# Chunk 1's decays read back from memory instead of built by TensorE, single loads per group, and a new instruction order

## The chip, the cores and the metric

One of the cores of a Trainium2 chip runs the kernel. The metric is the device time of one execution in microseconds (us). A core has five engines that run side by side, each through its own queue in order: TensorE (PE, matrix products), VectorE (DVE), ScalarE (ACT), GpSimd (POOL) and SyncE (SP), which here issues every DMA between memory and the on-chip buffers. Engines wait for each other on semaphores.

## The reference

Inputs are q, k, v and gates for 2 batches, 8 heads, 768 steps, head size 40. Three layers follow each other: a recurrent attention with a matrix state per head, and two small networks per token.

```python
for t in range(S):
    m_new = np.maximum(f_gate[:, :, t] + m, i_gate[:, :, t])
    f_stab = np.exp(f_gate[:, :, t] + m - m_new)
    i_stab = np.exp(i_gate[:, :, t] - m_new)
    C = f_stab * C + i_stab * outer(vt, kt)      # 40 x 40 state per head
    n = f_stab * n + i_stab * kt
    y[:, :, t] = sigmoid(o_gate[:, :, t]) * (C @ qt) / max(abs(n @ qt), 1)
# x: (2, 768, 320)
xn = (x - mean) / sqrt(var + 1e-06) * g_ln
x = x + relu(xn @ w_ch1) @ w_ch2                 # 320 -> 1280 -> 320
h = relu(x @ w_in)                               # 320 -> 1024
gate = sigmoid(conv3(h, conv_w))                 # along the sequence
out = (h * gate) @ w_out                         # 1024 -> 320
```

## The kernel before, in words

The 768 steps are cut into 6 chunks (c = 0 to 5) of 128. Within a chunk the recurrence is a masked attention: scores k·q (L488, two PSUM banks), multiplied by a decay matrix w (tile `wt`, 128 x 8 heads x 128) on DVE (L495), then the read-out (L504, L506), which adds the state `c` of the chunks before, applied to q times a decay `e` (tile `eg`). The state product of the next chunk (L541) uses k times `d`, the last column of w (POOL, L475). `attention(c, b)` records this for one chunk and batch b; "block" below is one such (c, b). Buffers rotate: 2 of `wt`, `eg` and `qt`, 3 of `vk` and `xy`.

The decays come from running sums of the gates. For chunk 0 they are made as the program starts. For chunks 1 to 5 `gates_rest` makes them in one go in tile `g80` (80 rows: 5 chunks x 16 heads and batches), and SP writes them to a scratch tensor `gd` in memory (L331, L332). How w and e are then made depends on the chunk:

- Chunks 0 and 1: PE builds log w in a PSUM bank by 6 matmuls per 4 heads, the "fill" (L434, L436, L438), and ACT takes exp of it in one instruction (L442).
- Chunk 1: PE spreads the rows of `g80` over 120 partitions by selector matrix `hsel` (L460), ACT takes exp (L464).
- Chunks 2 to 5: SP loads the rows of `gd` broadcast to 128 partitions, POOL masks them (L447), ACT takes exp head by head (8 x L451); e is loaded by three DMAs of 40 partitions and goes through one exp (L469). POOL multiplies q by e (L471).

After the read-out DVE normalizes (L516 to L533 give `xc`, ACT adds a small copy, L560), PE transposes (L567), ACT and DVE split the result into a high and a low part (`xth` L571, `xtl` L572). The first network is `f1_unit(c, u)`, u = 0 to 4: 16 matmuls L580 to L584, ACT's `uh` (L604), DVE's `ul` (L606), 12 matmuls L589 to L591. It needs both blocks of its chunk. The second network, `f2_unit`, does the same for chunk c - 3, with the convolution on ACT, DVE and POOL (L680 to L715). All weights come as 64-bit integers of doubles: SP loads 640 KB pieces into five staging buffers (`scr`, `stg`), ACT, DVE and POOL convert (L338 to L341) and split them into high and low parts (L364 to L386).

The order is written out by hand: `ORDER` lists the recorded operations by number, and each engine's queue is this list, cut to its own operations. A "-" is a dummy matmul on constants (L804, `warm`), which writes a PSUM bank that nothing reads. SP has 8 DMA slots in turn: a DMA is issued once the one issued 8 before it has landed, and once its buffer is free.

Of the kernel before, what the change touches and what calls it, by code (L numbers as in the profile page):

```python
# [8 lines left out]
F32 = mybir.dt.float32  # L9
# [21 lines left out]
10 8 41 9 5 11 6 30 - - 42 2 4 - 31 15 16 - 29 - 32 - 274 - 28 40 - 17 - 275 - - - - - 13 - - 3 86 39 7 - 18 - 14 20  # L31
273 53 157 93 107 - - 21 19 294 50 22 12 23 24 158 0 26 25 1 - 27 35 33 100 49 36 289 43 34 45 37 44 38 51 - 52 288 46
- - 87 56 47 88 89 48 54 280 286 55 - 90 67 58 59 57 60 68 91 114 61 62 94 63 - 159 69 64 70 95 92 380 108 287 71 65
109 121 72 66 96 73 97 - 160 173 101 74 - 162 - 75 381 102 163 - 237 - 98 76 172 - 238 165 171 161 80 77 166 239 78
164 81 240 99 167 83 241 - 84 - 379 - 82 116 - 242 168 128 169 79 276 115 179 85 170 281 103 277 117 104 300 110 278
282 295 283 105 243 123 106 111 296 244 122 135 301 279 124 245 297 284 400 246 290 402 112 302 403 247 175 285 291
113 129 118 292 130 131 142 248 293 137 249 125 303 298 119 250 132 126 304 120 251 127 133 - 508 - - - 509 143 252
255 149 305 144 253 306 174 299 136 180 134 254 308 176 145 187 177 138 178 146 150 307 404 321 139 322 147 323 414
152 151 148 182 153 256 382 140 324 392 261 181 309 310 325 257 141 262 154 311 258 188 330 326 312 263 259 507 155
327 313 189 194 260 383 318 264 267 401 314 319 405 386 268 315 389 320 391 156 409 265 269 316 394 528 343 266 412  # L40
393 270 317 344 384 395 345 333 328 407 346 271 334 331 347 329 390 335 348 336 410 332 272 337 388 338 417 422 341
408 415 423 387 339 416 342 190 340 396 183 191 349 413 530 406 531 385 350 411 397 398 420 192 425 355 424 418 399
351 356 419 195 352 426 196 193 197 357 353 716 421 208 428 354 717 427 198 361 358 429 184 199 185 200 367 209 510
431 186 520 210 362 215 211 201 432 368 212 433 363 434 364 430 369 435 213 370 511 436 437 214 373 513 532 512 542
517 440 515 438 229 518 374 443 439 529 444 441 519 516 445 442 514 455 375 359 446 523 456 376 526 452 522 202 527
447 521 360 203 533 453 217 365 715 448 216 457 366 449 204 541 471 538 450 371 536 472 534 218 451 473 372 539 454
537 219 540 461 535 458 544 462 377 459 545 463 550 543 474 378 460 548 475 220 476 549 464 524 467 477 465 469 525
468 230 466 478 221 736 232 470 551 231 546 205 479 483 739 553 738 552 484 547 206 480 554 207 485 486 481 902 555
233 903 556 495 222 234 557 235 558 728 559 560 561 718 562 563 224 564 223 565 568 740 571 566 489 750 572 569 567
737 573 570 583 490 584 574 731 719 225 729 580 491 730 496 722 575 721 226 727 585 901 482 726 581 497 576 725 589  # L50
741 498 723 487 590 577 492 724 599 488 746 600 578 601 742 745 582 493 602 749 744 743 591 494 751 603 747 604 752
758 499 748 753 579 756 720 757 586 732 500 587 733 734 920 588 501 227 735 502 754 228 592 755 503 605 593 504 606
594 236 759 607 608 505 923 760 922 761 621 506 622 623 637 595 624 596 611 597 638 625 598 626 762 612 627 628 631
613 629 614 639 632 763 640 765 615 633 641 616 764 642 617 643 618 827 634 766 914 767 619 768 904 769 770 771 772
647 924 779 773 780 774 934 781 776 775 782 648 620 921 777 649 783 905 663 778 788 664 630 912 925 784 911 916 910
789 679 915 913 785 790 909 917 813 930 791 680 786 657 936 814 933 937 650 787 815 792 699 935 927 651 816 929 793
794 652 817 658 918 818 653 795 846 654 919 797 796 940 700 655 659 926 801 660 665 609 932 666 938 673 667 906 939
907 668 674 908 669 928 931 610 635 644 645 636 646 670 671 656 681 675 672 682 676 661 683 701 684 702 689 685 662
686 865 690 687 677 691 692 688 693 678 694 695 705 696 697 703 802 706 803 704 798 804 707 799 698 807 800 708 808
825 805 709 806 941 710 711 712 884 826 943 713 819 942 828 829 714 944 830 809 811 810 831 812 844 945 832 845 946  # L60
833 947 847 1001 834 835 848 836 949 950 951 849 837 952 948 850 953 851 954 852 955 820 853 1020 958 956 854 957 863
821 959 960 822 967 855 961 968 969 856 962 963 973 838 964 965 987 966 839 988 989 990 970 991 840 992 864 971 841
823 972 866 867 882 883 868 869 976 885 824 977 870 842 978 974 871 857 975 872 1039 858 873 886 874 859 875 887 860
843 888 876 889 861 890 862 891 1058 892 877 893 878 879 894 880 983 985 984 895 986 896 993 897 898 994 999 995 996
1000 1012 1002 1003 1018 1004 1013 1005 1019 1014 1006 1015 881 1021 1007 1031 1008 1093 1032 1009 1022 1010 1011 1023
899 1024 900 1025 1026 1037 981 1027 1106 979 1038 982 1028 980 1075 1040 1079 1029 1041 1030 1042 997 1043 998 1044
1016 1045 1033 1046 1034 1017 1119 1047 1050 1051 1056 1052 1053 1057 1069 1076 1080 1077 1070 1059 1081 1078 1060
1082 1035 1061 1091 1062 1104 1063 1036 1064 1054 1065 1132 1071 1055 1066 1072 1092 1073 1094 1074 1105 1083 1095
1085 1117 1084 1107 1096 1086 1108 1118 1097 1146 1109 1120 1143 1130 1098 1110 1121 1131 1099 1111 1122 1155 1048
1100 1112 1144 1209 1049 1147 1145 1133 1168 1101 1148 1067 1134 1123 1166 1113 1135 1114 1124 1153 1136 1154 1192  # L70
1156 1125 1157 1210 1181 1137 1158 1068 1126 1138 1167 1127 1087 1159 1139 1088 1193 1169 1140 1089 1179 1170 1090
1160 1180 1171 1194 1223 1182 1161 1183 1236 1172 1212 1162 1237 1184 1173 1163 1195 1224 1174 1196 1249 1211 1197
1175 1225 1185 1176 1102 1226 1213 1198 1103 1186 1214 1115 1227 1116 1187 1215 1188 1238 1128 1199 1228 1189 1260
1239 1216 1164 1165 1240 1229 1217 1177 1200 1230 1178 1218 1201 1261 1190 1231 1250 1262 1219 1241 1191 1202 1232
1129 1242 1251 1141 1220 1252 1142 1253 1243 1203 1151 1233 1149 1152 1244 1204 1263 1150 1221 1222 1264 1245 1254
1246 1234 1207 1255 1265 1208 1205 1235 1256 1266 1206 1257 1267 1247 1258 1268 1248 1269 1259 1270 1271 1272 1274
1273 1275
"""


class Sched:

    LAT = {"A": dict(A=150, G=175, P=150, S=145, V=180), "V": dict(A=128, G=155, P=130, S=120, V=127),
# [786 lines left out]
```

## Time and profile before

| | us |
|---|---|
| median of 3 runs | 295.73 (293.85 to 297.31) |
| the profiled execution | 292.17 |
| its span, first to last instruction | 290.4 |
| PE busy in the span | 283.4 (98%) |
| DVE, ACT, POOL busy | 206.3, 179.0, 102.4 |

A page of the profile has the busy time of each engine, the chain of work that ended last, and groups of instructions by source line. PE's matmuls overlap each other, so that one shown with 0.28 us may follow its forerunner by 0.12; times between starts tell the rate. A view by windows gives busy times, TensorE's granted clock (1.00 is 2.4 GHz, 0.50 is 1.2 GHz) and DMA traffic in any stretch.

### The profile page before, as it was taken

Reading aid. Unit: us, or ns where it says so; the run is one execution under the profiler, and the core shown is the slowest. Engines: PE = TensorE matmul, PEld = TensorE weight load, DVE = VectorE, ACT = ScalarE, POOL = GpSimd, SP = SyncE. Lnnn points to the kernel's source line nnn. Section 1 sums busy time; section 2 is a strip of 40 time slices with the busy share of each in tenths; the row PEclk is TensorE's granted clock in tenths of the full one; section 3 lists DMA queues with packets and bytes.
Section 4 is the critical chain, followed back from the end, with each engine's and each line's share of the span. In section 5 each row is a group of like instructions: output and inputs, shape, how many; then the busy total and the mean of one; then the engine's idle time right before and its main releaser. Section 6 shows DMA issues by size and latency. Waiting matters only on the chain.

```text
span 290.4 us, 5879 instructions
## 1 busy us (share of the span) xinstructions
PE 283.4 (98%) x2206; PEld 269.0 (93%) x2209; DVE 206.3 (71%) x439; ACT 179.0 (62%) x409; POOL 102.4 (35%) x148
## 2 busy tenths in 40 slices
PE   8899999989999999999999999999999999999995
PEld 3685889979999999999999999999999999999995
DVE  4288987896798859469965678664165457899980
ACT  2376987878689638752685454463355447788861
POOL 6035767667537937500540000200000000444630
PEclk9997999999999999999999999999999999999999
DMA  7999888953698278022600010000100000010021
GB/s 180 279 380 271 279 234 290 292 208 83 208 313 292 59 240 273 27 56 96 212 14 1 2 47 1 0 2 0 47 0 2 0 0 3 1 47 1 2 90 45
DMA packets 13748, 33.27 MB, mean 115 GB/s; under 512 B 1783, under 2 KB 7688, under 8 KB 13720
## 3 DMA queue, kind: packets, MB, share of 16 engines
q1 hardware_dynamic: 13720, 32.90, 36.7%
q8 instruction: 17, 0.28, 0.4%
q14 instruction: 11, 0.09, 0.1%
HBM read 30.88 MB, written 2.01 MB: 113 GB/s over the span
## 4 chain that ended last, share of the span: by engine, by line
PE 85%; DMA 9%; ACT 1%; SPq 1%; issue 1%; DVE 1%; POOL 1%; POOLq 0%
PE bk L589 11%; PE bk L591 11%; PE bk L590 10%; PE bk L580 9%; PE bk L581 9%; PE bk L582 9%; PE bk L506 5%; PE bk L583 4%; PE bk L584 4%; DMA scr<-in_w_dram 4%; PE bk L488 4%; PE bk L504 3%; DMA vk<-in_vko_dram 3%; PE bk L567 3%; DMA wt<-gd 2%; PE bk L541 1%
## 5 line engine op out<-in xcount | busy, mean ns | idle before, releaser
L705 DVE SCALAR_TENSOR_TENSOR scr<-scr,cwr 128x256 f32<-128x256 f32 x70 | 35.8, 557 | 7.9 <-ACT scr L699 7.7
L680 POOL COPY scr<-scr 128x8 f32<-128x8 f32 (+1 forms) x21 | 6.0, 287 | 94.5 <-DVE scr L710 75.5
L589 PE MATMUL bk<-w2h,uh 128*128 128x320 f32 x120 | 38.3, 319 | 0.0
L591 PE MATMUL bk<-w2h,ul 128*128 128x320 f32 x120 | 37.2, 310 | 0.0
L590 PE MATMUL bk<-w2l,uh 128*128 128x320 f32 x120 | 37.1, 309 | 0.0
L580 PE MATMUL bk<-xth,w1h 128*128 128x256 f32 x120 | 35.7, 297 | 0.0
L581 PE MATMUL bk<-xth,w1l 128*128 128x256 f32 x120 | 33.8, 282 | 0.0
L582 PE MATMUL bk<-xtl,w1h 128*128 128x256 f32 x120 | 33.8, 282 | 0.0
L606 DVE SCALAR_TENSOR_TENSOR ul<-bk,uh 128x512 fp32r<-128x512 f32 x30 | 20.6, 687 | 17.5 <-ACT uh L604 17.3
L580 PE MATMUL bk<-rh,wih 128*128 128x256 f32 (+1 forms) x96 | 27.9, 291 | 0.0
L604 ACT ACTIVATE uh<-bk 128x512 fp32r<-128x512 f32 x30 | 17.9, 596 | 16.1 <-PE bk L584 13.9
L581 PE MATMUL bk<-rh,wil 128*128 128x256 f32 (+1 forms) x96 | 27.2, 284 | 0.0
L582 PE MATMUL bk<-rl,wih 128*128 128x256 f32 (+1 forms) x96 | 27.2, 283 | 0.0
L681 ACT ACTIVATE scr<-bk 128x512 f32<-128x512 f32 (+2 forms) x29 | 15.1, 522 | 17.5 <-PE bk L584 16.8
L506 PE MATMUL bk<-vk,wt 128*128 128x41 f32 x192 | 24.5, 270 | 0.0
L451 ACT ACTIVATE wt<-wt,bcol 128x128 f32<-128x128 f32 x64 | 21.4, 392 | 4.7 <-POOL wt L447 4.6
L506 PEld LDWEIGHTS bk<-vk,wt 128*128 128x128 f32 x192 | 24.1, 192 | 0.1
L341 POOL TENSOR_TENSOR scr<-scr 128x640 int32<-128x640 int32 x14 | 18.9, 1356 | 14.8 <-DVE scr L340 5.4
L589 PE MATMUL bk<-woh,uh 128*128 128x320 f32 x74 | 23.3, 315 | 0.0
L580 PEld LDWEIGHTS bk<-xth,w1h 128*128 128x128 f32 x120 | 22.6, 189 | 0.6
L589 PEld LDWEIGHTS bk<-w2h,uh 128*128 128x128 f32 x120 | 22.6, 189 | 0.4
L590 PE MATMUL bk<-wol,uh 128*128 128x320 f32 x74 | 22.9, 309 | 0.0
(192 smaller groups left out, 864.1 us busy)
## 6 DMA issues: line engine op xcount, KB each, us to landing
vk<-in_vko_dram SPq DMA_DIRECT2D x12, 528.0 KB
xy<-in_kq_dram SPq DMA_DIRECT2D x24, 192.0 KB
wt<-gd SPq DMA_DIRECT2D x8, 512.0 KB
scr<-in_w_dram SPq DMA_DIRECT2D x6, 640.0 KB
stg<-in_w_dram SPq DMA_DIRECT2D x4, 640.0 KB
scr<-in_win_dram SPq DMA_DIRECT2D x4, 640.0 KB
scr<-in_wout_dram SPq DMA_DIRECT2D x4, 640.0 KB
out_dram<-scr SPq DMA_DIRECT2D x12, 160.0 KB
```

The costliest lines, as they stand in the source:

```text
L341: op(G, 80 + 1.78 * n, [(rk, 0)], [(rk, 1)], lambda: gq.tensor_tensor(out=hi, in0=hi, in1=lo, op=ALU.add))
L451: lambda h=h: ac.activation(out=w[:, h, :], in_=w[:, h, :], func=AF.Exp, bias=bcol[:, c * 16 + r0 + h:c * 16 + r0 + h + 1]))
L506: pe.matmul(out=num[:, h * 41:(h + 1) * 41], lhsT=w[:, h, :], rhs=v1[:, h * 41:(h + 1) * 41], start=(c == 0), stop=(c == 0 or h == min(3 * ...
L580: pe.matmul(out=pv, lhsT=wh[:, k, fs], rhs=hi(k), start=(k == 0), stop=False)
L581: pe.matmul(out=pv, lhsT=wl[:, k, fs], rhs=hi(k), start=False, stop=False)
L582: pe.matmul(out=pv, lhsT=wh[:, k, fs], rhs=lo(k), start=False, stop=False)
L589: pe.matmul(out=a, lhsT=hi(b), rhs=wh[:, k, :], start=first, stop=False)
L590: pe.matmul(out=a, lhsT=hi(b), rhs=wl[:, k, :], start=False, stop=False)
L591: pe.matmul(out=a, lhsT=lo(b), rhs=wh[:, k, :], start=False, stop=last)
L604: op(A, da(512, True), [pk], [hk], lambda: ac.activation(out=uh[i], in_=pb, func=AF.Relu))
L606: lambda: ve.scalar_tensor_tensor(out=ul[i], in0=pb, scalar=0.0, in1=uh[i].bitcast(F32), op0=ALU.max, op1=ALU.subtract))
L705: ve.scalar_tensor_tensor(out=cvt()[:, j], in0=h[:, j, :, k:k + 128], scalar=cw_t[:, k, f0 + j:f0 + j + 1], in1=cvt()[:, j], op0=ALU.mult, ...
```

## The change

Chunk 1 now goes the way of chunks 2 to 5: w and e are loaded from `gd` (all conditions `c < 2` become `c == 0`). `hsel`, the second pair of `gp` and `bp` (inputs of the fill) and their making are dropped. For all chunks e is loaded by one DMA per group of three heads, to all 120 partitions; its source is three rows of `gd`, each repeated 40 times. The keys and queries of a block come by one load of 112 partitions instead of two of 48. Some durations that only served to find the order differ, and `ORDER` is a new list. Lines shift: L434 becomes L429, L447 L442, L451 L446, L469 L453, L488 L472, L567 L551, L580 L564, L804 L788.

```diff
--- before.py
+++ after.py
@@ -28,53 +28,53 @@
 ORDER = """
-10 8 41 9 5 11 6 30 - - 42 2 4 - 31 15 16 - 29 - 32 - 274 - 28 40 - 17 - 275 - - - - - 13 - - 3 86 39 7 - 18 - 14 20
...
+4 8 36 9 2 10 6 5 13 37 - - 28 - 26 25 3 - 27 - 153 - 81 - 11 0 - 7 12 1 - 265 - - - 95 14 - - - 15 44 16 - 152 - -
...
@@ -188,7 +188,6 @@
-    hsel = T([32, 17 * 40], "hsel")
...
@@ -270,20 +269,17 @@
...
-    op(G, 1500, ["ident"], ["hsel"],
-       lambda: gq.tensor_copy(out=hsel.rearrange("p (r d) -> p r d", d=40), in_=ident[0:32, 0:17].unsqueeze(2).to_broadcast([32, 17, 40])))
...
@@ -302,11 +298,11 @@
-        for t, src, sk, key in ((gp[k], g[0:16, :], gkey, ("gp", k)), (bp[k], i[0:16, :], ki, ("bp", k))):
-            op(A, da(L), [sk], [key], lambda t=t, src=src: ac.activation(out=t[0:16, :], in_=src, func=AF.Copy))
-            op(V, 200, [sk], [key],
-               lambda t=t, src=src: tv(out=t[32:48, :], in0=src, in1=t[0:16, :].bitcast(F32), op=ALU.subtract))
         if k == 0:
+            for t, src, sk, key in ((gp, g, gkey, "gp"), (bp, i, ki, "bp")):
+                op(A, da(L), [sk], [key], lambda t=t, src=src: ac.activation(out=t[0:16, :], in_=src, func=AF.Copy))
+                op(V, 200, [sk], [key],
+                   lambda t=t, src=src: tv(out=t[32:48, :], in0=src, in1=t[0:16, :].bitcast(F32), op=ALU.subtract))
@@ -412,7 +408,7 @@
-        load(v, vko[c, b], [("vk", vkey, x) for x in "vko"], 128 * VKO * 4.5)
+        load(v, vko[c, b], [("vk", vkey, x) for x in "vko"], 128 * VKO * 4)
         v1 = v[:, 0:VW]
         kk_ = v[:, VW:VW + KW]
         ot = v[:, VW + KW:VW + KW + DM]
...
@@ -421,11 +417,10 @@
         q, qk = qt[i % 2], ("qt", i % 2)
         e, ek = eg[i % 2], ("eg", i % 2)
         xt, xkk = xy[i % 3], ("xy", i % 3)
-        for h2 in range(2):
-            load(xt[64 * h2:64 * h2 + 48], kq0[c, b, h2], (xkk, h2), 48 * 4096)
-        if c < 2:
+        load(xt[0:112], kq0[c, b], [(xkk, h2) for h2 in range(2)], 112 * 4096)
+        if c == 0:
             for h2 in range(2):
-                wb = 6 if c else 4 + (2 * b + h2) % 3
+                wb = 4 + (2 * b + h2) % 3
                 bk = ("bank", wb)
                 wp = bank[wb].rearrange("p (h t) -> p h t", h=4)
 
@@ -433,15 +428,15 @@
                     r = r0 + h2 * 4
                     pe.matmul(out=wp, lhsT=identb, rhs=negm, start=True, stop=False)
                     for j in range(4):
-                        pe.matmul(out=wp[:, j, :], lhsT=sel[:, r + j:r + j + 1].to_broadcast([128, 128]), rhs=gp[c],
+                        pe.matmul(out=wp[:, j, :], lhsT=sel[:, r + j:r + j + 1].to_broadcast([128, 128]), rhs=gp,
                                   start=False, stop=False)
-                    pe.matmul(out=wp, lhsT=bp[c], rhs=sel[:, r:r + 4].unsqueeze(2).to_broadcast([128, 4, 128]),
+                    pe.matmul(out=wp, lhsT=bp, rhs=sel[:, r:r + 4].unsqueeze(2).to_broadcast([128, 4, 128]),
                               start=False, stop=True)
-                op(P, 216 * 2 + 4 * 97, [("gp", c), ("bp", c), "negm", "identb", "sel"], [bk], fw, act=0.8)
+                op(P, 216 * 2 + 4 * 97, ["gp", "bp", "negm", "identb", "sel"], [bk], fw, act=0.8)
                 op(A, da(512, True), [bk], [(wk, h2 * 4 + j) for j in range(4)],
                    lambda wp=wp, h2=h2: ac.activation(out=w[:, 4 * h2:4 * h2 + 4, :], in_=wp, func=AF.Exp))
         r1 = (c - 1) * 16 + r0
-        if c >= 2:
+        if c:
             load(w, gd[r1:r1 + 8, :].partition_broadcast(128), [(wk, h) for h in range(8)], 128 * 4096, reads=["gd"])
             op(G, 1060, [], [(wk, h) for h in range(8)],
                lambda: gq.affine_select(out=w, in_=w, pattern=[[0, NH], [1, L]], compare_op=ALU.is_ge, fill=NEG,
@@ -452,21 +447,10 @@
                                              bias=bcol[:, c * 16 + r0 + h:c * 16 + r0 + h + 1]))
         if c:
             load(q, q3t[c, b], qk, 120 * 3 * L * 4)
-            if c == 1:
-                gk, gb = pbank("sm")
-
-                def feg():
-                    for g in range(3):
-                        pe.matmul(out=gb[0:120, g * L:(g + 1) * L], rhs=g80[0:32], start=True, stop=True,
-                                  lhsT=hsel[:, 40 * (r1 + 3 * g):40 * (r1 + 3 * g + 3)])
-                op(P, 3 * 224 + 390, ["g80", "hsel"], [gk], feg, act=0.5)
-                op(A, da(384, True), [gk], [(ek, j) for j in range(3)],
-                   lambda: ac.activation(out=e, in_=gb[0:120, 0:384].rearrange("p (g t) -> p g t", g=3), func=AF.Exp))
-            else:
-                gsrc = gd[r1:r1 + 9, :].rearrange("(g j) t -> j g t", j=3)
-                for j in range(3):
-                    load(e[40 * j:40 * j + 40], gsrc[j].partition_broadcast(40), (ek, j), 2 * 40 * 3 * L * 4, reads=["gd", "gd8"])
-                op(A, da(384), [], [(ek, j) for j in range(3)], lambda: ac.activation(out=e, in_=e, func=AF.Exp))
+            for g in range(3):
+                gsrc = gd[r1 + 3 * g:r1 + 3 * g + 3, :].unsqueeze(1).to_broadcast([3, 40, L])
+                load(e[:, g, :], gsrc, (ek, g), 120 * L * 4, reads=["gd", "gd8"])
+            op(A, da(384), [], [(ek, j) for j in range(3)], lambda: ac.activation(out=e, in_=e, func=AF.Exp))
             op(G, dg(384), [(ek, j) for j in range(3)], [qk],
                lambda: gq.tensor_tensor(out=q, in0=q, in1=e, op=ALU.mult))
         if c < NC - 1:
```

The first place is PE from the transpositions of chunk 0 to the first matmul of the first network. Before (bk is a PSUM bank, `xc` a normalized block; further dummies are left out at "..."):

```order
L567 MATMUL bk_133<-ident,xc_104 128x128 x3
L541 MATMUL bk_132<-vk_85 120x123 x3
L567 MATMUL bk_134<-ident,xc_105 128x128 x3
L804 LDWEIGHTS const-bfloat16-1.0
L804 MATMUL bk_138<-const-bfloat16-1.0 128x512
...
L312 MATMUL bk_133<-ident,early_69 128x80
L434 LDWEIGHTS identb
L434 MATMUL bk_137<-ctmp,identb 128x512
L436 MATMUL bk_137<-xth_117 128x128 x4
L438 MATMUL bk_137<-xth_117 128x512
L460 MATMUL bk_134<-g_79,hsel 120x128 x3
...
L580 MATMUL bk_131<-xth_116,w1h 128x256
```

And with the change:

```order
L551 MATMUL bk_133<-ident,xc_104 128x128 x3
L788 LDWEIGHTS const-bfloat16-1.0
L788 MATMUL bk_137<-const-bfloat16-1.0 128x512
...
L551 MATMUL bk_132<-ident,xc_103 128x128 x3
...
L308 MATMUL bk_132<-ident,early_69 128x80
L564 MATMUL bk_130<-xth_115,w1h 128x256
L565 MATMUL bk_130<-xth_115,w1l 128x256
```

The fills and `hsel` products of chunk 1 are gone; 23 dummies now stand between the two transpositions (none before) and 7 behind the second (4 before). Up to the first matmul of the first network there are 71 dummies instead of 36.

The second place is SP from the write of `gd` to the end of chunk 1's reads, with the change (before, no read of `gd` was among them, and the first `wt` load stood nine rows behind the write):

```order
L327 DMA gd<-g_78 80x128
L328 DMA gd<-g_78 1x128
L251 DMA scr<-in_w_dram 128x1280 x2
L251 DMA vk_83<-in_vko_dram 128x1056
L251 DMA stg_119<-in_w_dram 128x1280
L251 DMA wt_90<-gd 128x1024
L251 DMA eg_88<-gd 120x1x128
L251 DMA wt_91<-gd 128x1024
L251 DMA eg_89<-gd 120x1x128
L251 DMA eg_88<-gd 120x1x128
L251 DMA eg_89<-gd 120x1x128 x2
L251 DMA eg_88<-gd 120x1x128
```

Eight loads of chunk 1's decays now stand between the weights of the first network and the first load of the second network's; the last of the six `eg` loads is the third one of `eg_88`.

The third place is ACT in the same stretch, with the change (`uh` is the first network's output, `stg` and `scr` are weights):

```order
L446 ACTIVATE wt_90<-wt_90,bcol 128x128 x6
L588 ACTIVATE uh_123<-bk_130 128x512
L446 ACTIVATE wt_91<-wt_91,bcol 128x128 x2
L457 ACTIVATE d_92<-wt_90 128x8
L453 ACTIVATE eg_88<-eg_88 120x384
L446 ACTIVATE wt_91<-wt_91,bcol 128x128 x6
L453 ACTIVATE eg_89<-eg_89 120x384
L457 ACTIVATE d_93<-wt_91 128x8
L360 ACTIVATE w1h<-stg_119 128x2x256
L588 ACTIVATE uh_124<-bk_131 128x512
L334 ACTIVATE stg_120<-stg_120 128x640
```

Where before two exps of 512 columns per block stood, there are now eight of one head each, and the exp of `eg_88` stands ahead of six of them, of weight conversions, and of what chunk 1's normalized blocks need from ACT.

## Rows read from the trace of the kernel before

**Rows 1.** Windows: us; busy PE, PEld, DVE, ACT, POOL; clock; DMA share; GB/s.

```profile
24.00:25.00 1.00, 1.00 (x3) 0.37 (x2) 1.00 (x5) 0.48 (x1) 1.00 (x1) 0.50 1.02 272
30.00:40.00 10.00, 9.88 (x75) 8.62 (x76) 9.50 (x13) 9.25 (x20) 8.73 (x7) 1.00 0.82 251
50.00:60.00 10.00, 10.00 (x84) 10.00 (x84) 9.14 (x21) 6.95 (x13) 6.45 (x6) 1.00 0.97 324
260.00:280.00 20.00, 20.00 (x147) 20.00 (x146) 18.96 (x31) 15.97 (x33) 10.80 (x11) 1.00 0.02 8
```

**Rows 2.** Chain of waits in order of time: start us, us, what.

```profile
34.93 1.09 PE bk L488 x16
51.65 6.95 DMA wt<-gd
66.70 0.31 PE bk L580
287.12 0.44 ACT scr L737
```

**Rows 3.** Timeline of PE: start us, us, line, operation, count, idle before.

```profile
0.84 6.63 PE L804 MATMUL bk<-const-bfloat16-1.0 128*128 128x512 bf16 x18 [0.84 <-PEq L860]
30.09 0.91 PE L460 MATMUL bk<-g,hsel 32*120 32x128 f32 x6 [0.18 <-DVE xtl L572]
30.94 0.39 PE L434 MATMUL bk<-ctmp,identb 128*128 128x512 bf16 x1
31.92 0.91 PE L460 MATMUL bk<-g,hsel 32*120 32x128 f32 x6
32.76 0.39 PE L580 MATMUL bk<-xth,w1h 128*128 128x256 f32 x1
43.25 0.82 PE L804 MATMUL bk<-const-bfloat16-1.0 128*128 128x512 bf16 x3 [0.16 <-issue]
44.86 0.31 PE L589 MATMUL bk<-w2h,uh 128*128 128x320 f32 x1
46.61 0.38 PE L504 MATMUL bk<-c,qt 120*128 120x123 f32 x2
61.65 0.44 PE L567 MATMUL bk<-ident,xc 128*128 128x128 f32 x2 [0.36 <-DVE xc L533]
62.76 0.33 PE L567 MATMUL bk<-ident,xc 128*128 128x128 f32 x1 [0.67 <-ACT xc L560]
```

**Rows 4.** Timeline of ACT, in the same columns.

```profile
18.80 0.69 ACT L364 ACTIVATE w1h<-scr 128x512 fp32r<-128x512 f32 x1 [1.18 <-POOL scr L341]
20.05 0.79 ACT L338 ACTIVATE scr<-scr 128x640 f32<-128x640 f32 x1
20.75 0.78 ACT L339 ACTIVATE scr<-scr 128x640 int32<-128x640 uint32 x1
28.87 0.80 ACT L339 ACTIVATE stg<-stg 128x640 int32<-128x640 uint32 x1 [0.66 <-DMA stg<-in_w_dram]
33.55 0.81 ACT L339 ACTIVATE scr<-scr 128x640 int32<-128x640 uint32 x1 [0.18 <-DMA scr<-in_w_dram]
67.02 1.26 ACT L451 ACTIVATE wt<-wt,bcol 128x128 f32<-128x128 f32 x4
```

**Rows 5.** DMA issues of the page: line, operation, count, KB each.

```profile
vk<-in_vko_dram SPq DMA_DIRECT2D x12, 528.0 KB
xy<-in_kq_dram SPq DMA_DIRECT2D x24, 192.0 KB
wt<-gd SPq DMA_DIRECT2D x8, 512.0 KB
scr<-in_w_dram SPq DMA_DIRECT2D x6, 640.0 KB
eg<-gd SPq DMA_DIRECT2D x24, 60.0 KB
```

**Rows 6.** Windows view, the columns of Rows 1, while six `eg` loads run alone.

```profile
62.00:63.00 1.00, 0.33 (x3) 0.24 (x3) 1.00 (x2) 1.00 (x5) 0.84 (x3) 1.00 0.42 130
```

## What the change does to the time: a prediction

> **What bounds the kernel now.** I read the windows first, then the chain of waits, then the timelines of PE, ACT and SP for the first 70 us. In the windows the reader is to see two stages. From 50 us on PE is busy but for one us near 62, 10.00 of 10 and 20.00 of 20 us in the windows shown, late on with DVE at 18.96 of 20 behind it and the granted clock at 1.00 (2.4 GHz) [rows 1]. Before that PE shares the bound with the loads: the DMA engines are 0.82 to 0.97 busy at 251 to 324 GB/s [rows 1], and PE fills gaps with dummies. The chain has its last links at 287.12, where PE hands over to the output copy [rows 2].
>
> The timeline of PE gives the marks that I use: first matmul of the first network at 32.76, read-out of chunk 1 from 46.61, transpositions of chunk 1 at 61.65 and 62.76 with 0.36 and 0.67 us of waiting [rows 3], and the first network's start on chunk 1 at 66.70 [rows 2]. From there to 287.12 are 220.4 us of PE work without a gap worth naming. The change leaves that work alone but for its order, so **the question is when chunk 1 reaches the first network**.
>
> **What goes.** PE loses four fills of 0.98 us (30.94 to 31.92) and two selector products of 0.85 (30.09 to 30.94) [rows 3], 5.6 us together. Two fills and both products stood ahead of 32.76, two fills behind it. ACT loses four exps of 512 columns, DVE and POOL some small preparations; they were beside PE's work and I give nothing for them.
>
> **What comes, ahead of the first network.** 35 more dummies at 0.215 us each (three in 0.82, the last of which shows 0.39 [rows 3]) make 7.5 us. Were all else as before, the first network would start at 32.76 - 3.7 + 7.5 = 36.6; dummies that only fill waits bring that down, by some 2 us at most, to 34.6. Now the chain: ACT reaches the small copy that the first transposition needs behind a conversion of `stg_120`. In the old queue 7,016 KB, summed along SP's rows, stand up to the load whose conversion starts at 28.87, freed by its landing [rows 4]; in the new one 7,092 KB stand up to `stg_120`. So: 29.1 landed, 0.8 conversion, 0.25 copy, transposition at 30.2, 0.3 for it, 23 dummies 4.9, second transposition 0.5, 7 dummies 1.5. **First network at 37.4**, 4.6 later. The far end: 18 dummies at the start took 6.63 us rather than 3.9 [rows 3], and in one stretch the clock stood at 0.50 (1.2 GHz) while dummies ran [rows 1]; if the 23 meet that, 2.8 more.
>
> PE then needs from 32.76 to 46.61, 13.85 us [rows 3], to chunk 1's read-out. The new queue holds there two fills less (2.0), 24 first-network matmuls (0.12 each) and 12 second-layer ones (0.146, from twelve in 44.86 to 46.61 [rows 3]) more, and one dummy more: 16.7. PE arrives at 54.1.
>
> **The read.** Up to `wt_90` SP's new queue holds 11,872 KB; 8,376 KB had landed at 33.5 before [rows 4, 5], and the 1,360 KB from 28.9 to 33.5 came at 303 GB/s. 3,496 KB more at that rate take 11.8 us: 45.3. At 251 and 324 GB/s [rows 1] it is 47.8 and 44.5. (The old first reads of `gd` took 6.95 us from issue [rows 2], with fewer loads ahead.) `wt_91` adds 512 KB, 1.75 us.
>
> The six `eg` loads in between are the unknown. While six old ones ran alone, the 16 engines were 0.42 busy at 130 GB/s [rows 6]: 6.7 engine-us for 254 rows of 512 bytes, 26 ns a row. A new load has 120 such rows. On all engines six cost 1.2 us; if each of the three source rows keeps to one engine, 40 rows take it 1.04 us, and six 6.2, during which every later load waits for these engines' share. The old source began with a dimension of 40 and kept less than half the engines busy; the new begins with 3. I take the upper end: **last `eg` at 45.3 + 1.75 + 6.2 = 53.3**; the lower is 48.3.
>
> The Trainium skill (page "DMA: Bandwidth & Descriptors", section "Why a DMA increments its semaphore by 16 and not by 1") says that a DMA is spread over the largest number of engines, up to 16, that divides the slowest dimension of both sides. By that rule the old loads had 10 engines and the new ones have 3, which would give the upper end; that less than half were busy agrees, and no run here shows the new form yet.
>
> **ACT behind it.** The exp of `eg_88` stands in ACT's queue ahead of everything that follows. Between it and the copy for chunk 1's normalized block come 8 exps at 0.29, 8 conversions at 0.70, two triple copies at 1.25 [rows 4], and five small ones, some 1.7 together: 12.1 us. 53.3 + 0.4 + 12.1 = 65.8; two copies, an exp and a first-layer output 1.1, two more exps and the two `xth` copies 1.4 with the transpositions between, DVE's last `xtl` 0.6: **first network on chunk 1 at 69.0**. PE would be there sooner: from 46.61 to 61.65 it took 15.0 with 40 and 36 matmuls of the two layers; with 16 and 12 it takes 8.7, so it arrives at 62.8 and waits some 4 us. That is the wait that takes the place of 1.03 us.
>
> One group of scores, 1.09 us [rows 2], stood ahead of 66.70 and now stands behind. **The sum**: 69.0 + 1.1 - 66.7 = +3.4 us on the profiled 292.17 (290.4 of span and 1.8 around it), 295.6. The median of the runs is 295.73, 3.6 above that execution, so I put the median at **299.1**.
>
> Costed at nothing: two more masks on POOL and 16 short exps less four long ones on ACT, counted where ACT binds; wider key loads, 12 of 448 KB for 24 of 192 KB [rows 5], whose 768 KB are in the byte sums early and lie under an idle DMA late (0.02 busy [rows 1]); without that cover they would cost 2.6 us in all. The `eg` loads of the later chunks meet idle engines too.
>
> **Rivals.** *The new `eg` loads are as wide as the old.* For it: same bytes, as many rows. Then `eg` is there at 48.3, ACT comes to it only after the first eight exps, near 51.5, and all behind moves up by 1.8: +1.6 us, 297.3, within 1%. Chance 0.30.
>
> *The removed PE work counts.* Against: the marks say that PE waits for loads and ACT. It decides if ACT has the copy of chunk 1's second block done by 60 rather than 66.9, which needs its conversions to run ahead in the waits I do not see. PE then goes 34.6 + 16.7 + 8.7 = 60.0, first network on chunk 1 at some 62: 62 + 1.1 - 66.7 = -3.6, 292.1, faster. Chance 0.10.
>
> *The tail turns into a wait.* The last convolution group's first matmul stands 72 closing matmuls from the end, 10.5 us at 0.146, where 114 or 16.6 us stood before, while DVE is 18.96 of 20 busy [rows 1]. A backlog of DVE as old would show as up to 4 us on top: 303. Chance 0.15, on the forecast's side. That the table is not used is excluded: the dummies stand where it has them.
>
> **How the numbers follow.** About 1%, 3 us, is what a measurement can tell from no change. Forecast 0.42 and tail 0.15 are slower by more: 0.57. The wide loads and a remainder of the forecast, within 1%: 0.33. Faster 0.10. The range leaves out the fast case below and the tail's end with a half-speed spell above: 294.2 to 303.2.
>
> **What would show it.** Right: first network at 36 to 39; the last `eg_88` near 53 with ACT waiting for it; PE waiting 2 to 5 us around 63 to 67; 220 us without a gap behind. Wrong: a landing of `eg` before 50, no PE wait ahead of the transpositions of chunk 1, or gaps in the last 20 us.

## The result: no difference that the runs can tell

The changed kernel takes 297.2 us (median of 20 runs, 293.92 to 303.38), the kernel before 296.15 (20 runs). The ratio, which leaves disturbed executions out and so is not the quotient of the medians, is 1.0062, 95% interval 1.0033 to 1.0091: 0.6% or 1.8 us, where 299.1 was forecast. Both kernels were run again, each time with a new comparison: the changed one gave 1.0021 [0.998, 1.0061] and 1.0080 [1.0034, 1.0127], the kernel before, against itself, 1.0055 [1.0005, 1.0105] and 1.0017 [0.9958, 1.0075]. So the unchanged kernel, too, shows half a per cent in one of two comparisons. The three ratios of the changed kernel have the mean 1.0054, the two of the unchanged one 1.0036. What is left is some 0.2%. All three ratios of the changed kernel lie within 1%, though the interval of the last one reaches 1.3%.

The profiled execution of the changed kernel took 296.33 us (span 294.5), 4.16 more than that of the kernel before, and this needs care (below). Its windows, in the columns of [rows 1]:

```profile
30.00:40.00 10.00, 9.76 (x43) 4.89 (x43) 6.17 (x15) 7.47 (x18) 5.35 (x10) 0.83 1.02 392
50.00:60.00 10.00, 10.00 (x91) 9.68 (x90) 7.53 (x15) 9.93 (x25) 7.05 (x8) 1.00 0.94 277
260.00:280.00 20.00, 20.00 (x157) 20.00 (x156) 15.99 (x29) 15.65 (x32) 10.71 (x13) 1.00 0.04 15
```

From 30 to 40 the DMA engines are full and move 392 GB/s where they moved 251 [rows 1], PE is at a mean clock of 0.83, and at the end PE is again without a gap.

The chain of waits from 14 to 38 us, in the columns of [rows 2]:

```profile
14.35 14.91 DMA stg<-in_w_dram
29.27 0.77 ACT stg L335
30.05 0.15 ACT xc L544
30.24 0.33 PE bk L551
30.57 6.69 PE bk L788 x23
37.26 0.34 PE bk L551 x3
```

The chain that the prediction drew is there: a weight load lands at 29.27, ACT converts it, then copies the small block, the transposition follows, and 23 dummies stand ahead of the second one. The timeline of PE, in the columns of [rows 3]:

```profile
30.24 0.33 PE L551 MATMUL bk<-ident,xc 128*128 128x128 f32 x1 [2.02 <-ACT xc L544]
30.41 6.85 PE L788 MATMUL bk<-const-bfloat16-1.0 128*128 128x512 bf16 x23
38.98 0.36 PE L564 MATMUL bk<-xth,w1h 128*128 128x256 f32 x1
55.13 0.45 PE L488 MATMUL bk<-c,qt 120*128 120x123 f32 x2
65.58 0.62 PE L551 MATMUL bk<-ident,xc 128*128 128x128 f32 x3 [0.43 <-DVE xc L517]
66.56 0.62 PE L551 MATMUL bk<-ident,xc 128*128 128x128 f32 x3 [0.36 <-DVE xc L517]
68.77 0.28 PE L564 MATMUL bk<-xth,w1h 128*128 128x256 f32 x1
69.69 0.39 PE L566 MATMUL bk<-xtl,w1h 128*128 128x256 f32 x1 [0.53 <-DVE xtl L556]
```

First network at 38.98, chunk 1's read-out at 55.13, first network on chunk 1 at 68.77. Ahead of the latter PE waits 0.43 and 0.36, just behind its start 0.53: 1.32 us, all for DVE. DVE itself works without a wait from 55 us on, so here its queue sets the pace. The timeline of ACT has no bracket, so no wait, at the exps of chunk 1's matrices (L446) and decays (L453), and POOL masks the first matrix at 44.98 without one:

```profile
29.27 0.77 ACT L335 ACTIVATE stg<-stg 128x640 int32<-128x640 uint32 x1 [2.97 <-DMA stg<-in_w_dram]
47.86 1.85 ACT L446 ACTIVATE wt<-wt,bcol 128x128 f32<-128x128 f32 x6
51.41 0.51 ACT L453 ACTIVATE eg<-eg 120x384 f32<-120x384 f32 x1
```

```profile
44.98 1.56 POOL L442 TENSOR_SCALAR_AFFINE_SELECT wt<-wt 128x1024 f32<-128x1024 f32 x1
```

**Three profiles of each kernel.** Two marks cut the span in three: the first matmul of the first network on chunk 0 and that on chunk 1 (66.63 in the first profile before, the piece at 66.70 in [rows 2]). Lengths in us, read from the timelines of PE:

```
                     start   to chunk 1   to PE's last matmul
before               32.76     33.87        220.46
  again              37.29     33.60        220.45
  third              35.56     33.55        221.75
  mean               35.20     33.67        220.89
changed              38.98     29.79        222.41
  again              40.01     29.79        221.76
  third              37.42     29.84        221.64
  mean               38.80     29.81        221.94
difference           +3.60     -3.86        +1.05    sum +0.79
```

The middle length hardly moves within a kernel, the start by 4.5 us. Three more profiles widen this. `eg_three` (below), which does the same as the changed kernel up to there, starts at 36.12. `xy_one` (below), which has the old order, has 34.19, 32.69 and 222.47. So the two kernels' starts overlap and the size of the +3.60 is uncertain by some us. The last length moves by 2 us within the old order (220.45 to 222.47), so the +1.05 is not told from scatter.

What makes the middle shorter can be counted. The groups of instructions between the marks (count, busy us, mean ns, idle before) have 48 score matmuls in the first profile before and 32 in the first one of the changed kernel:

```profile
L488 PE MATMUL bk<-xy 40*128 40x128 f32 x48 | 3.9, 287 | 0.0
L472 PE MATMUL bk<-xy 40*128 40x128 f32 x32 | 2.3, 285 | 0.0
```

One score group (1.1 us) has moved behind the second mark, and two fills (2.0 us) are gone. The rest of the 3.86, some 0.8 us, is not taken apart. (The 30.3 us of two expectations below are the same length, read to a matmul half a us later.) The profile from which the forecast was made had the earliest start of the three.

### The profile page after: what moved, and what is told of

The parts are those of the page before. It is cut to its first block, busy times and chain, and to the rows that moved or that the text cites. A ratio compares the mean times of both kernels' runs of the same rounds, so it can differ in the third digit from the quotient of the medians.

```text
span 294.5 us, 5891 instructions
## 1 busy us (share of the span) xinstructions
PE 285.0 (97%) x2208; PEld 265.1 (90%) x2208; DVE 204.5 (69%) x435; ACT 182.6 (62%) x419; POOL 102.3 (35%) x149
## 4 chain that ended last, share of the span: by engine, by line
PE 68%; DMA 13%; DVE 7%; ACT 6%; issue 2%; SPq 1%; POOL 1%; ACTq 0%; POOLq 0%
PE bk L573 9%; PE bk L575 9%; PE bk L574 9%; PE bk L564 7%; PE bk L565 7%; PE bk L566 7%; DMA stg<-in_w_dram 7%; PE bk L568 4%; PE bk L567 4%; DMA scr<-in_w_dram 3%; PE bk L490 3%; PE bk L551 2%; PE bk L788 2%; PE bk L472 2%; PE bk L488 2%
## 5 line engine op out<-in xcount | busy, mean ns | idle before, releaser
L689 DVE SCALAR_TENSOR_TENSOR scr<-scr,cwr 128x256 f32<-128x256 f32 x70 | 32.5, 509 | 14.0 <-ACT scr L683 12.4
L664 POOL COPY scr<-scr 128x8 f32<-128x8 f32 (+1 forms) x21 | 6.9, 330 | 86.2 <-DVE scr L694 82.7
L564 PE MATMUL bk<-xth,w1h 128*128 128x256 f32 x120 | 35.3, 294 | 0.0
L588 ACT ACTIVATE uh<-bk 128x512 fp32r<-128x512 f32 x30 | 17.7, 592 | 18.0 <-PE bk L568 14.6
L564 PE MATMUL bk<-rh,wih 128*128 128x256 f32 (+1 forms) x96 | 27.9, 291 | 0.0
L446 ACT ACTIVATE wt<-wt,bcol 128x128 f32<-128x128 f32 x80 | 26.4, 389 | 1.9 <-POOL wt L442 1.9
L337 POOL TENSOR_TENSOR scr<-scr 128x640 int32<-128x640 int32 x14 | 18.1, 1296 | 15.0 <-ACT scr L335 7.0
L575 PEld LDWEIGHTS bk<-w2h,ul 128*128 128x128 f32 x120 | 22.5, 188 | 0.9 <-DVE ul L590 0.9
L566 PEld LDWEIGHTS bk<-xtl,w1h 128*128 128x128 f32 x120 | 22.6, 188 | 0.7 <-DVE xtl L556 0.7
L564 PEld LDWEIGHTS bk<-xth,w1h 128*128 128x128 f32 x120 | 22.6, 188 | 0.6
```

The costliest lines, as they stand in the source:

```text
L337: op(G, 80 + 1.78 * n, [(rk, 0)], [(rk, 1)], lambda: gq.tensor_tensor(out=hi, in0=hi, in1=lo, op=ALU.add))
L446: lambda h=h: ac.activation(out=w[:, h, :], in_=w[:, h, :], func=AF.Exp, bias=bcol[:, c * 16 + r0 + h:c * 16 + r0 + h + 1]))
L564: pe.matmul(out=pv, lhsT=wh[:, k, fs], rhs=hi(k), start=(k == 0), stop=False)
L566: pe.matmul(out=pv, lhsT=wh[:, k, fs], rhs=lo(k), start=False, stop=False)
L575: pe.matmul(out=a, lhsT=lo(b), rhs=wh[:, k, :], start=False, stop=last)
L588: op(A, da(512, True), [pk], [hk], lambda: ac.activation(out=uh[i], in_=pb, func=AF.Relu))
```

## Experiments

Four repeats and eight variants were run; each ratio is to the kernel before, run at the same time.

**The kernels again.** No edit.

> The kernel before, unchanged, profiled a second time. Its first profiled execution took 292.17 us, less than the 20 timed ones (median 296.15). If the gap of 4.2 us between the two profiles is partly that execution's luck, this one comes out 1 to 3 us longer, with a difference to be seen ahead of 33 us (clock, first loads); if the gap is the change, span 290 to 291 again. Time ratio 1.00 within 0.5%.

> The kernel before a third time. Two profiles had the first network at 32.8 and 37.3 us and 254.3 and 254.1 us from there to TensorE's last matmul. Expected: the second figure 254 again, the first anywhere between 32 and 38; the ratio between 0.995 and 1.006.

> The changed kernel once more. If the change costs 0.6% and the comparison resolves that, the ratio is 1.003 to 1.009 again; if the comparison of two such kernels is itself uncertain by half a per cent (the unchanged kernel run under a new name came out at 1.0055), it can fall anywhere from 0.999 to 1.010. From the start of the first network to TensorE's last matmul this program should take 252 to 253 us as in its three other profiles, against 254.1 in both profiles of the kernel before; the start itself 36 to 39 us.

> The changed kernel a third time. Two profiles had the first network at 39.0 and 40.0 us and 252.2 and 251.6 us from there to the last matmul (30.3 us from network to network). Expected: these lengths again, the start between 36 and 40 us; the ratio between 1.000 and 1.009.

The ratios stand above, the spans were 294.7, 294.2, 294.9 and 292.2 us. So two executions of the same kernel differ by 4.3 us of span (290.4 and 294.7), as much as the two profiles that were to be compared, and all of it lies ahead of the first network. The traces show two causes.

In the second profile of the kernel before PE waits longer for the keys, and its granted clock then stands at 0.50 from 12 to 20 us (rows at the end):

```profile
10.67 1.80 PE L488 MATMUL bk<-xy 40*128 40x128 f32 x14 [1.13 <-DMA xy<-in_kq_dram]
37.29 0.39 PE L580 MATMUL bk<-xth,w1h 128*128 128x256 f32 x1
```

The fills of chunk 0 come slower, and ACT takes their last exp (L442) at 19.96, where it was 15.19 in the first profile. From there the lateness only travels on. The conversion that began at 28.87 in the first profile, freed by the landing of its load [rows 4], begins at 32.91 without a wait. ACT in the first profile (one row) and the second (two rows):

```profile
15.19 0.60 ACT L442 ACTIVATE wt<-bk 128x512 f32<-128x512 f32 x1 [0.29 <-PE bk L438]
19.96 0.60 ACT L442 ACTIVATE wt<-bk 128x512 f32<-128x512 f32 x1 [1.14 <-PE bk L438]
32.91 0.77 ACT L339 ACTIVATE stg<-stg 128x640 int32<-128x640 uint32 x1
```

In the third profile the last exp comes at 16.59, but the same conversion waits for its load until 31.46:

```profile
16.59 0.60 ACT L442 ACTIVATE wt<-bk 128x512 f32<-128x512 f32 x1 [0.39 <-PE bk L438]
31.46 0.79 ACT L339 ACTIVATE stg<-stg 128x640 int32<-128x640 uint32 x1 [1.17 <-DMA stg<-in_w_dram]
```

In the changed kernel, too, both play a part. In its third profile the 23 dummies (22 are recorded) take 5.19 us instead of 6.85, and the network starts 1.56 us sooner, though they begin at the same time:

```profile
30.51 5.19 PE L788 MATMUL bk<-const-bfloat16-1.0 128*128 128x512 bf16 x22
```

Some expectations were missed: the second profile before was 4.3 us longer, not 1 to 3, the second start of the changed kernel was 40.01, outside 36 to 39, with 251.6 us behind it instead of 252 to 253, and in the third profile before 255.3 us lie behind the start instead of 254.

**The removed TensorE work, in the new order** (`fills_kept`).

```diff
 program: that of the kernel before (fills, selector products, two key loads)
-ORDER of the kernel before
+ORDER of the changed kernel; fills and products of chunk 1 near its masks and exps
```

> The program of the kernel before (fills and decays of chunk 1 by TensorE, two loads per group) in the new order with its 75 dummies; the fills stand where the new order has the masks. Theory A (the removed TensorE work counts, the start is late for other reasons): the first network starts at 37 to 40 us or later by what is filled ahead of it, 254 us or more lie between it and the last matmul, and the time is 2 to 5 us over the changed kernel. Rival (the removed work lay beside waits of the same length): within 1 us of the changed kernel.

1.0165 [1.0092, 1.0238], median 300.2 us; the changed kernel had 1.0021 [0.998, 1.0061] against the same runs of the kernel before. The first network starts at 37.81, and 33.64 us lie between the marks. In the table it is 29.81 with the same order and the reads. So the new order alone does not shorten the middle; the removed work does, by 3.8 us, and that is what stands there. (It is not the make-up of the table's 3.86, since the old order has other work between the marks.) The view of instruction groups for PE in that stretch (count, busy us, mean ns, idle before) has three fills and one group of selector products; at 0.89 a fill and 0.91 they make 3.6:

```profile
L436 PE MATMUL bk<-xth 128*128 128x128 f32 x12 | 2.2, 308 | 0.0
L438 PE MATMUL bk<-xth 128*128 128x512 f32 x3 | 1.3, 432 | 0.0
L434 PE MATMUL bk<-ctmp,identb 128*128 128x512 bf16 x3 | 1.2, 390 | 0.0
L460 PE MATMUL bk<-g,hsel 32*120 32x128 f32 x6 | 0.9, 284 | 0.0
```

The rival (the removed work lay beside waits) falls. The key loads and the shape of the decay loads are old here as well; two runs below show no price of either.

**The reads, in the old order** (`order_old`).

```diff
 program: that of the changed kernel
-ORDER of the changed kernel
+ORDER of the kernel before; chunk 1's reads of gd behind its write, their masks and exps moved
```

> The changed program (chunk 1 read back, one load per group) in the order of the kernel before; only the reads of chunk 1 (right behind the write of the decays), their masks and exponentials and what hangs on them get new places. Theory A (the new order's lateness in front of the first network is what eats the saving): the first network starts near 30 to 33 us as in the kernel before less its two fills and two decay groups, and the time is 2 to 4 us under the kernel before. Theory B (the reads need the new order): ahead of the weights' loads they push the weights back, and their 16 exponentials (0.31 us apart on ScalarE) stand between the weights' conversions, so TensorE waits for chunk 1 or for weights by 50 us: time 1 to 5 us over the kernel before.

1.0278 [1.0182, 1.0374], median 306.95 us, more than theory B had it. Its profiled execution took 310.03 us, and much of its lateness lies ahead of the reads (its lines are one lower). SP issues no load between 14.47 and 31.79 us, the DMA engines stand at 0.01 from 24 to 32, PE's granted clock is 0.50 there, and the first read of `gd` is issued at 37.94:

```profile
24.00:32.00 8.00, 8.00 (x37) 7.41 (x37) 4.26 (x15) 3.97 (x7) 0.18 (x1) 0.50 0.01 3
```

Behind that comes the wait of theory B. ACT stands 4.95 us at an exp of `wt`, whose mask waits for the read; the first output of the network, `uh`, is behind it in the queue, and PE waits 6.73 us for that:

```profile
45.91 1.57 ACT L445 ACTIVATE wt<-wt,bcol 128x128 f32<-128x128 f32 x5 [4.95 <-POOL wt L441]
51.14 0.57 ACT L587 ACTIVATE uh<-bk 128x512 fp32r<-128x512 f32 x1
```

```profile
51.76 0.64 PE L572 MATMUL bk<-w2h,uh 128*128 128x320 f32 x1 [6.73 <-ACT uh L587]
```

With the runs above the four combinations are, as ratios to the kernel before (the diagonal as means of the repeats):

```
                     old order        new order
fills by TensorE      1.0036           1.0165
reads of gd           1.0278           1.0054
```

The new order costs some 1.3%, and the reads pay 1.1% back in it (the intervals reach 0.3% to 1% to either side). The reads in the old order cost 2.8%, but how much of that is theory B's wait and how much the stall ahead of it, is not shown: the old order with other places for the reads might do better.

**The shape of the decay loads** (`eg_three`).

```diff
-for g in range(3): load(e[:, g, :], gd[r1+3g:r1+3g+3, :].unsqueeze(1).to_broadcast([3, 40, L]), ...)
+gsrc = gd[r1:r1 + 9, :].rearrange("(g j) t -> j g t", j=3)
+for j in range(3): load(e[40*j:40*j + 40], gsrc[j].partition_broadcast(40), ...)
```

> The changed kernel with its decay loads in the shape of the kernel before (three loads of 40 partitions per group instead of three of 120 with a slow dimension of 3). Theory of the prediction (narrow loads hold the reads back): the last decays land 3 to 5 us earlier, ScalarE and TensorE wait less around 63 to 67, and the end comes 1 to 2 us earlier. Rival from the trace of the changed kernel (no exponential of chunk 1's decays waited for its load): end unchanged within 0.5 us, and the only wait on such a load (1.19 us at 74.6, chunk 2) goes or stays without moving TensorE.

1.0018 [0.9975, 1.0061]. Between the marks 29.81 us, as with the new loads: the rival that nobody waits for them. In the changed kernel (first row) the loads of the new shape run alone from 43 to 46. Loads of the old shape run all but alone in the kernel before (second row), in the busiest half us of the window of [rows 6], whose mean of 0.42 takes in time before they ran:

```profile
43.00:46.00 3.00, 3.00 (x23) 2.58 (x22) 2.09 (x4) 2.93 (x7) 2.23 (x2) 1.00 0.22 64
62.75:63.25 0.50, 0.49 (x4) 0.49 (x5) 0.50 (x2) 0.50 (x3) 0.34 (x2) 1.00 0.71 211
```

0.22 of 16 engines are 3.5 at 64 GB/s, 0.71 are 11.4 at 211 GB/s. The rule quoted from the Trainium skill (page "DMA: Bandwidth & Descriptors", section "Why a DMA increments its semaphore by 16 and not by 1") gives 3 and 10 engines; these traces agree in the ratio, and both shares come out some 15% high. At 64 GB/s the six loads, 368,640 bytes, take 5.8 us (6.2 forecast). So the loads are as narrow as forecast, and nobody waits for them: the last of their packets, by the trace's records the only ones of 512 bytes at that time, ends at 48.7, and ACT comes to them at 51.41. SyncE is longer at it, 8.05 us for five issues against 5.04 with the old shape (second row):

```profile
36.72 8.05 SPq L251 DMA_DIRECT2D eg<-gd  x5
34.56 5.04 SPq L251 DMA_DIRECT2D eg<-gd  x5
```

**The dummies** (`dummies_12`, `dummies_0`).

```diff
-transposition, 23 dummies, transposition, 7 dummies, first network
+transposition, 12 dummies, transposition, 7 dummies, first network     (dummies_12)
+transposition, transposition, first network                            (dummies_0)
```

> The changed kernel with 12 dummy matmuls instead of 23 between the two transpositions of chunk 0. In its trace xc of the first-in-queue batch is ready at 35.2 us, while the 23 dummies (6.85 us, from 30.4) hold TensorE until 37.1. Theory A (dummies in the way): the second transposition moves from 37.1 to about 35.3, the first network from 39.0 to about 37.2, and the end by 1 to 1.9 us: about 295.6 against 297.2. Theory B (they keep the clock): TensorE is at half clock longer and the first network runs in it: no gain, or up to 2 us lost. Theory C (chunk 1 sets the end anyway): the network starts 1.9 us earlier, but TensorE then waits as much longer at chunk 1's read-out or transpositions (54 to 67 us): end unchanged within 0.5 us.

> The changed kernel without any of the 23 dummies between and the 7 behind the transpositions of chunk 0. Theory A (in the way): nothing more than with 12 left, since the copy of xc at 35.2 us then sets the second transposition: first network at 36.5 to 37.2, end 1 to 2 us earlier. Theory B (they keep the clock): TensorE stands idle from 30.4 to 35.2, the granted clock is at half when the first network starts, and its first 3 to 4 us of matmuls take twice as long: first network past its first unit no earlier than in the changed kernel, end 0 to 3 us later than it. Theory C: end unchanged within 0.5 us, the gain lost at 54 to 67 us.

With 12: 1.0029 [0.9978, 1.0080], start 37.37, 29.75 us between the marks. With all 23 it was 37.42 to 40.01, and 36.12 in `eg_three`; the second transposition now waits 1.04 and 0.47 us for `xc`. Whether 11 dummies cost anything is not shown. With none: 1.0130 [1.0065, 1.0196], 298.04 us: theory B, clear of `eg_three` in the same comparison. PE idles 3.67 us; then the network's matmuls take 0.41 us instead of 0.28 and stand at a granted clock of 0.50 (1.2 GHz) for 8 us, and 33.22 us lie between the marks, 3.4 more (its lines are one lower):

```profile
34.41 0.69 PE L550 MATMUL bk<-ident,xc 128*128 128x128 f32 x2 [3.67 <-DVE xc L516]
37.12 0.56 PE L563 MATMUL bk<-xth,w1h 128*128 128x256 f32 x1
43.84 0.41 PE L564 MATMUL bk<-xth,w1l 128*128 128x256 f32 x1
44.86 0.28 PE L564 MATMUL bk<-xth,w1l 128*128 128x256 f32 x1
```

```profile
36.00:44.00 8.00, 7.00 (x38) 6.56 (x39) 2.34 (x6) 4.23 (x8) 4.85 (x5) 0.50 0.72 274
```

**An earlier start** (`chain_first`, `chain_gap`), the attempt to keep the saving and get the start back.

```diff
 VectorE, ScalarE, chunk 0's second block:
-readout, conversions, gate, statistics, conversions, xc, conversions; copy of xc behind a weight's conversion
+readout, gate, statistics, xc, conversions; copy of xc ahead of it                       (chain_first)
+readout, conversion, gate, statistics, xc, conversions; copy of xc behind two of them    (chain_gap)
 TensorE: 8 and 4 dummies (chain_first), 2 and 3 (chain_gap) in place of 23 and 7
```

> The changed kernel with chunk 0's second output chain (readout, gate, statistics, xc, its copy) put ahead of the weights' conversions on VectorE and ScalarE, and 8 and 4 dummies in place of 23 and 7. In the changed kernel ScalarE stood 2.97 us for a weight load ahead of a copy of xc, and VectorE 1.84 us behind it. Theory A (the chain waits behind conversions that wait for loads): both transpositions by 32 us, first network at 32 to 34 us, the end 2 to 4 us earlier than the changed kernel. Theory B (the weights themselves arrive no earlier): TensorE waits 2 to 6 us for w2 at the network's first second-layer matmuls (38 to 45 us), end within 1 us of the changed kernel.

> The changed kernel with four instructions of chunk 0's second output chain (gate, two of statistics, xc) moved on VectorE into the 1.84 us in which it waited for a conversion of ScalarE, its copy and transposition behind them, and 2 and 3 dummies in place of 23 and 7; no conversion is moved behind a wait (that is the difference to the run in which the chain went ahead of all of them). Theory A (every us by which the first network starts earlier is kept, since 30.3 us lie between the two networks in all profiles of the changed program): first network at 33 to 34 us instead of 39 to 40, no new wait behind it, the end 3 to 5 us earlier: 292 to 294 us. Theory B (ScalarE's conversions set the pace): TensorE waits 2 to 5 us between 37 and 46 us at the first second-layer matmuls, and the end stays within 1 us of the changed kernel. Half clock at the start of the network may take 1 us of A.

1.0224 [1.0160, 1.0288] and 1.0119 [1.0037, 1.0200]. In the same comparisons the changed kernel had 1.0021 [0.998, 1.0061] and 1.0080 [1.0034, 1.0127]: the first is slower than it, the second not faster, though the network starts at 34.58 and 36.02. The middle grows to 42.0 and 35.2 us. In the first, ACT waits 3.54 us for the moved `xc` and converts the weights behind it later, and PE waits 4.44 us at the second layer:

```profile
32.64 0.26 ACT L544 ACTIVATE xc<-xc 128x64 f32<-128x64 f32 x1 [3.54 <-DVE xc L517]
33.70 0.77 ACT L335 ACTIVATE stg<-stg 128x640 int32<-128x640 uint32 x1
45.60 0.57 ACT L588 ACTIVATE uh<-bk 128x512 fp32r<-128x512 f32 x1
```

```profile
46.22 0.41 PE L573 MATMUL bk<-w2h,uh 128*128 128x320 f32 x1 [4.44 <-ACT uh L588]
```

In the second, ACT reaches the first `uh` (L588, first row) at 42.02 without a wait, its queue being full up to there. In the changed kernel (second row) it is there at 42.40 after waiting 1.19 us for PE, which began 3 us later:

```profile
42.02 0.58 ACT L588 ACTIVATE uh<-bk 128x512 fp32r<-128x512 f32 x1
42.40 0.60 ACT L588 ACTIVATE uh<-bk 128x512 fp32r<-128x512 f32 x1 [1.19 <-PE bk L568]
```

PE then waits 0.89, 0.91 and 2.14 us:

```profile
48.18 0.41 PE L575 MATMUL bk<-w2h,ul 128*128 128x320 f32 x1 [0.89 <-DVE ul L590]
55.96 0.46 PE L488 MATMUL bk<-c,qt 120*128 120x123 f32 x2 [0.91 <-DVE wt L479]
68.36 0.55 PE L551 MATMUL bk<-ident,xc 128*128 128x128 f32 x3 [2.14 <-ACT xc L544]
```

These are the waits of theory B: a start that PE alone gets is taken back by queues behind it, ACT's above all. But theory B had the end within 1 us of the changed kernel, and the first attempt is some 6 us over it: moving the chain also made the conversions later. Fewer dummies may have a part in both (the clock is 0.68 and 0.50 from 32 to 36), which was not tested apart. Theory A, and my expectation of 292 to 294 us, fall.

**The key loads alone** (`xy_one`).

```diff
 kernel before, its order
-for h2 in range(2): load(xt[64*h2:64*h2 + 48], kq0[c, b, h2], (xkk, h2), 48 * 4096)
+load(xt[0:112], kq0[c, b], [(xkk, h2) for h2 in range(2)], 112 * 4096)
```

> The kernel before, in its own order, with one part of the change alone: the keys and queries of a group in one load of 112 partitions (448 KB) instead of two of 48 (384 KB together). Theory of the prediction (no term: hidden): within 0.3% of the kernel before. Rival 1 (a load on more partitions comes in sooner): the second scores start 0.5 to 1.5 us earlier than 9.0 to 10.7 us and so does the first network. Rival 2 (17% more bytes in a stretch in which the transfers are never idle): the weights' loads come 0.2 us later per group, the first network 0.5 to 1 us later.

1.0040 [1.0001, 1.0080], hardly more than the unchanged kernel's 1.0036. The second scores wait 2.25 us and start at 10.65, so they are not sooner:

```profile
10.65 1.38 PE L486 MATMUL bk<-xy 40*128 40x128 f32 x16 [2.25 <-DMA xy<-in_kq_dram]
```

That the part is hidden is borne out as far as half a per cent can tell.

## Why the prediction was right, and where not

- **Range and sign of the terms**: 297.2 lies in 294.2 to 303.2. That says little, since the time of the unchanged kernel, 296.15, lies there too; the forecast itself, 299.1, is 1.9 too high. A later start, a shorter middle and one score group moved behind are there. The likeliest case, slower by over 1%, did not come.
- **The later start** (4.6 us, to 37.4): it came at 38.98, 40.01 and 37.42, through the chain that was drawn (the load landed at 29.27, 29.1 forecast). The far end, dummies at half clock, is in good part what happened: 23 dummies took 6.85 us instead of 4.9 in the first profile. But the kernel before starts at 35.2 in the mean of three profiles, not at 32.76. The term is +3.6 by these means, with the scatter told above. A start that hangs on the landing of loads and on PE's clock was read from one execution as a property of the kernel.
- **The read**: `wt_90` was forecast for 45.3 and masked at 44.98 without a wait. **This is the step that failed: "last `eg` at 53.3".** The width was right and its price nearly (5.8 us for 6.2), but the six loads do not follow `wt_91` at 47.05. At 392 GB/s, not 303, the 4096-byte packets of both matrices have ended by 43.5, and the last `eg` has landed by 49. That is the sign of being wrong that was named (before 50), and close to the lower bound of 48.3, though not by its reason.
- **ACT behind it, PE waiting some 4 us**: did not come. ACT takes the exps when it gets to them, DVE holds `xc`, and PE waits 1.32 us. That the first network on chunk 1 was forecast for 69.0 and found at 68.77 (67.26 and 69.80 in the other profiles) is partly luck: PE arrives at 65.2, not at 62.8, because the start and the read-out came later and the stretch took 10.0 us, not 8.7. By lengths, the middle was put 2.3 us shorter, and is 3.9 shorter.
- **What is left behind** (+1.1 for a score group): the group did move; +1.05 in the means agrees, but is within the scatter. The gaps of the tail that one rival feared are not there, PE is at 20.00 of 20 from 260 to 280.
- **The sum**: +4.6 - 2.3 + 1.1 = +3.4 forecast, +3.6 - 3.9 + 1.05 = +0.8 measured. The rival "as wide as the old" had the right number, 297.3, by a mechanism that is wrong. The rival "the removed PE work counts", put at 0.10, had the mechanism of the middle, as `fills_kept` shows: PE and not the reads sets its length. It had the middle too short (34.6 to 62, 27.4 us for 29.8) and the start too early (34.6 for 38.8), so its 292.1 did not come.

Still open: whether the change costs nothing or half a per cent, how much of the later start belongs to the new order and how much to the scatter of executions, and what the reads would cost in a better old order.

## What to carry to other kernels

Cut the span at marks that every execution has, and compare lengths between marks from several profiles: here the middle repeats within 0.3 us in three profiles and tells a saving of 3.9 (1.1 of it work that only moved), while the totals scatter by 4. Work taken from the busiest engine counted in full here where that engine set the pace (3.8 us for 3.6), but an order that makes room for its replacement has its own price, which running each half alone can show. A slow load has a price only if its consumer gets there first, so work out both times before the price goes into the sum.

## What was not expected

Dummies are worth their place: without 30 of them the first network ran 8 us at a granted clock of 0.50, and the middle was 3.4 us longer. The same kernel's first network started at 32.76, 35.56 and 37.29 us in three executions. In the latest of them PE had waited 0.47 and 1.13 us for keys, and the granted clock stood at 0.50 from 12 to 20 us, where the other two had 1.00:

```profile
12.00:20.00 8.00, 7.67 (x29) 5.83 (x28) 1.29 (x2) 2.52 (x6) 0.72 (x1) 0.50 1.03 357
```

```profile
12.00:20.00 8.00, 7.34 (x54) 6.14 (x54) 3.34 (x8) 4.57 (x10) 2.69 (x3) 1.00 1.03 350
```

The first row is the latest start, the second the third execution, in the columns of the windows above.
